# Dividing one early weight load and the input transpose before it in a TensorE-bound kernel

## The chip, the cores and the metric

The kernel runs on one core of one Trainium2 chip. The metric is the device time of one execution, in microseconds (us). The profile's span is the time from the first to the last recorded instruction of one profiled execution; here it is 1.3 to 1.4 us shorter than the device time of the same run.

## The reference

```python
g = sigmoid((x * gate_w).sum(-1))              # one gate per row
a = ssm(x)        # Bu = x @ B_bar^T (complex); h_t = Lam_bar*h_{t-1} + Bu_t; y = 2 Re(h @ C^T) + x*Dskip
b = gelu(x @ w1 + b1) @ w2 + b2
out = g * a + (1 - g) * b                      # x: 2048 x 640, w1: 640 x 1728, all bf16
```

For this change only `x @ w1` counts. The contraction length 640 is five row blocks of 128 (k = 0 to 4 in the code; the text counts them from one to five).

## The kernel before

The kernel works on four quarters of 512 rows. It opens with a pass of 42 matmuls over the first 1024 columns of W1, for the first quarter: all eight column blocks of row block one, then of row block two, and so on, into eight banks of PSUM, the memory that TensorE writes its results to. This order lets TensorE start as soon as the first row block of W1 and the first 128 columns of x are there, while the rest is still on its way. (The first two input blocks are loaded plainly and transposed on TensorE; the other three are transposed by DMA.) All of these loads are issued by one queue, SP, in this order:

```python
load("xna", "sp", "l_xna", ...)              # x, first two blocks, 256 KB
w1load(0, "sp", 1)                           # W1 row block one, 256 KB (128 x 1024)
w1load(1, "sp", 1.3)
xtrans(0, range(KN, KN + 1), 1.6, 0.8)       # DMA transpose of input block three, 128 KB
w1load(2, "sp", 2)
xtrans(0, range(KN + 1, KD), 3, 1.3)         # DMA transpose of input blocks four and five, 256 KB
w1load(3, "sp", 4)                           # W1 row block four
w1load(4, "sp", 5)                           # W1 row block five
# ... then: columns 1024 to 1727 of W1 in two parts ("w1_r0", "w1_r1"), the two B transposes, ...
```

The first pass asks for row block k only when it gets there:

```python
seq = [(k, jf) for k in range(KD) for jf in range(NW)]          # NW = 8 column blocks
# ... two small exceptions in the order of row blocks one and two cut ...
for k, jf, h in steps:
    op(f"m1_0_{jf}_{k}_{t0}", "pe", d_mm(t1 - t0), XK0[k] + [("w1", k)], [("bank", jf)], f_mm, ...)
```

Ahead of it, seven matmuls on a constant ("warm") and eight small transposes on TensorE are run.

## Time and profile before

| what | value | view |
|---|---|---|
| time | 213.02 us (212.69 to 213.04, 3 runs) | times |
| span of the profiled run | 211.5 us | page |
| TensorE busy | 208.6 us, 99% | page, part 1 |
| chain of waits that ended last | 99% TensorE | page, part 4 |
| TensorE's only stop in the first pass | 0.5 us ahead of one weight load | waits |

From the page of the kernel before: busy time by engine, the DMA row of the 40 slices (each digit is the busy share in tenths), and the shares of the chain that ended last.

```profile
PE 208.6 (99%) x1102; PEld 104.7 (50%) x1102; DVE 190.1 (90%) x240; ACT 103.3 (49%) x177; POOL 4.2 (2%) x12
...
DMA  6999999999400020063364000006752000005251
...
PE 99%; DVE 0%; issue 0%
```

TensorE is the limit. The DMA engines are nearly full for the first quarter of the run (ten of 40 slices) and have room in most of what follows, so the opening is the place to look for a late load.

The waits of TensorE's weight loads between 5 and 25 us, kernel before (total us, times, longest):

```profile
PEld ps L631 <- issue: 0.5, 1, 0.5
```

The chain that ended last, in order of time (start, us, what), kernel before. L407 are the warm-up matmuls, L419 the transposes on TensorE, L631 the first pass, L653 the following W1 matmuls, L696 the B projection:

```profile
0.78 2.93 PE ps L407 x7
3.71 0.03 issue
3.74 1.04 PE ps L419 x8
4.78 2.56 PE ps L631 x13
7.34 0.06 PE ps L438
7.40 2.81 PE ps L631 x13
10.20 0.06 issue
10.27 3.61 PE ps L631 x16
13.88 5.40 PE ps L653 x25
19.27 10.79 PE ps L696 x50
```

Row blocks four and five are the last 16 matmuls of L631. They start after a stop. Nothing on the later lines of this stretch stops TensorE again. The queue's issues in that stretch (start, us it took, instruction; L333 is a plain load, L340 a DMA transpose):

```profile
3.70 0.64 SPq L333 DMA_DIRECT2D W1sb<-in_B_w_dram  x1
4.38 1.26 SPq L340 DMA_TRANSPOSE xT<-in_A_x_dram  x1
5.69 2.10 SPq L333 DMA_DIRECT2D W1sb<-in_B_w_dram  x4
7.83 6.58 SPq L340 DMA_TRANSPOSE BT<-in_A_B_re_dram  x1
```

The two-block transpose takes 1.26 us of the queue, and row block four is the first of the four loads behind it.

### The profile page before, as it was taken

What the parts mean: (1) busy time and instruction counts of PE and PEld (TensorE: products, weight loads), DVE (VectorE), ACT (ScalarE), POOL (GpSimd) and SP (SyncE); (2) the same over time, 40 slices, a digit from 0 to 9 for tenths busy, and PEclk for the clock granted to TensorE, in tenths of its full rate; (3) what the DMA queues carried; (4) which work ended last, traced back from release to release, by engine and by line L of the source; (5) the groups of instructions that cost most, each with busy time, mean ns of one, the idle gap of its engine ahead of it and who ended that gap; (6) DMA issues with size and microseconds to landing.
All of it is one profiled execution on the core that took longest, in us unless ns stands there. A gap on an engine that the chain in (4) does not pass through costs nothing.

```text
span 211.5 us, 2743 instructions
## 1 busy us (share of the span) xinstructions
PE 208.6 (99%) x1102; PEld 104.7 (50%) x1102; DVE 190.1 (90%) x240; ACT 103.3 (49%) x177; POOL 4.2 (2%) x12
## 2 busy tenths in 40 slices
PE   8999999999999999999999999999999999999996
PEld 4444444444564444444464444444456444567775
DVE  2599999999999998999999999899999999499744
ACT  2489556679850353556680063456660037623330
POOL 1000000120000000000010000000010000000000
DMA  6999999999400020063364000006752000005251
GB/s 169 273 257 181 159 201 282 309 184 224 83 0 3 0 50 0 0 117 76 58 55 118 3 0 0 0 2 112 98 106 108 0 3 0 0 0 105 68 140 64
DMA packets 48424, 19.08 MB, mean 90 GB/s; under 512 B 41372, under 2 KB 47132, under 8 KB 48412
## 3 DMA queue, kind: packets, MB, share of 16 engines
q1 hardware_dynamic: 46752, 17.59, 39.1%
q0 software_dynamic: 1600, 1.32, 4.4%
q8 instruction: 8, 0.13, 0.3%
q10 hardware_dynamic: 60, 0.01, 0.1%
q14 instruction: 4, 0.03, 0.1%
HBM read 8.41 MB, written 2.63 MB: 52 GB/s over the span
## 4 chain that ended last, share of the span: by engine, by line
PE 99%; DVE 0%; issue 0%
PE ps L653 22%; PE ps L696 20%; PE ps L920 20%; PE ps L969 15%; PE ps L783 7%; PE ps L832 5%; PE ps L631 4%; PE ps L407 1%; PE ps L674 1%; PE ps L931 1%; PE ps L419 0%; PE ps L797 0%; DVE W1sb L866 0%; PE ps L438 0%
## 5 line engine op out<-in xcount | busy, mean ns | idle before, releaser
L653 PE MATMUL ps<-xT,W1sb 128*128 128x512 bf16 x220 | 48.1, 379 | 0.0
L736 DVE TENSOR_TENSOR_SCAN W<-atab,V 128x1280 bf16<-128x1280 f32 x16 | 44.3, 2811 | 0.3
L696 PE MATMUL ps<-xT,BT 128*128 128x512 bf16 x200 | 43.8, 379 | 0.0
L920 PE MATMUL ps<-Gl,W2sb 128*128 128x512 bf16 (+1 forms) x234 | 42.7, 344 | 0.0
L660 ACT ACTIVATE Gl<-ps,cols 128x512 bf16<-128x512 f32 x44 | 29.9, 694 | 15.5 <-PE ps L653 15.5
L653 PEld LDWEIGHTS ps<-xT,W1sb 128*128 128x128 bf16 x220 | 21.5, 98 | 26.0
L969 PE MATMUL ps<-Hb,CT 128*128 128x512 bf16 x150 | 32.9, 379 | 0.0
L920 PEld LDWEIGHTS ps<-Gl,W2sb 128*128 128x128 bf16 x234 | 22.9, 98 | 19.3
L705 ACT ACTIVATE U<-ps 128x512 bf16<-128x512 f32 x40 | 23.7, 596 | 15.6 <-PE ps L696 15.6
L696 PEld LDWEIGHTS ps<-xT,BT 128*128 128x128 bf16 x200 | 19.5, 98 | 23.8 <-ACT Gt L682 0.4
L938 ACT ACTIVATE E1T<-ps,cols 128x512 bf16<-128x512 f32 (+1 forms) x18 | 9.5, 624 | 36.0 <-PE ps L931 36.0
L969 PEld LDWEIGHTS ps<-Hb,CT 128*128 128x128 bf16 x150 | 14.4, 98 | 18.0 <-DVE Hb L488 0.3
L977 ACT ACTIVATE E2T<-ps 128x512 bf16<-128x512 f32 x15 | 9.1, 604 | 13.6 <-PE ps L969 13.6
L783 PE MATMUL ps<-W2sb,Gl 128*128 128x320 bf16 x104 | 14.8, 299 | 0.0
L606 DVE SCALAR_TENSOR_TENSOR trf<-xn,gwb 128x640 bf16<-128x640 bf16 x16 | 13.2, 823 | 0.4
L488 DVE TENSOR_TENSOR Hb<-Hb,V 128x1280 bf16<-128x1280 bf16 x16 | 12.5, 821 | 0.3
L488 DVE TENSOR_TENSOR V<-V,W 128x1280 bf16<-128x1280 bf16 x16 | 12.5, 821 | 0.3
L488 DVE TENSOR_TENSOR V<-mr,U 128x2560 bf16<-128x2560 bf16 x8 | 11.9, 1492 | 0.3
L783 PEld LDWEIGHTS ps<-W2sb,Gl 128*128 128x128 bf16 x104 | 10.1, 98 | 4.3 <-issue 0.3
L488 DVE TENSOR_TENSOR Hb<-c,W 128x2560 bf16<-128x2560 bf16 x8 | 11.9, 1491 | 0.2
L488 DVE TENSOR_TENSOR V<-s,W 128x2560 bf16<-128x2560 bf16 x8 | 11.9, 1484 | 0.0
L488 DVE TENSOR_TENSOR W<-mi,U 128x2560 bf16<-128x2560 bf16 x8 | 11.9, 1484 | 0.0
(91 smaller groups left out, 150.6 us busy)
## 6 DMA issues: line engine op xcount, KB each, us to landing
W2sb<-in_B_w_dram SPq DMA_DIRECT2D x1, 2080.0 KB, 9.1
out_dram<-xn SPq DMA_DIRECT2D x3, 640.0 KB, 4.8
W1sb<-in_B_w_dram SPq DMA_DIRECT2D x5, 256.0 KB, 4.2
xn<-in_A_x_dram POOLq DMA_DIRECT2D x2, 640.0 KB, 7.4
trf<-grow SPq DMA_DIRECT2D x3, 256.0 KB, 5.1
xn<-in_A_x_dram SPq DMA_DIRECT2D x1, 640.0 KB, 7.3
W1sb<-in_B_w_dram SPq DMA_DIRECT2D x1, 480.0 KB, 5.6
out_dram<-W1sb SPq DMA_DIRECT2D x3, 160.0 KB, 1.8
```

What stands on the lines that cost most here:

```text
L488: return inc("dve", nc.vector.tensor_tensor(out=o, in0=a, in1=b, op=o_))
L606: t = inc("dve", nc.vector.scalar_tensor_tensor(out=scr[:, :], in0=xn[q % 2][:, c, :], scalar=1.0, in1=gwb[:, :], op0=ALU.mult, op1=ALU.mu ...
L653: t = nc.tensor.matmul(PS[bank][:, :], W1sb[:, k, jf * 128:(jf + 1) * 128], xT[q][:, k, :], start=(k == 0), stop=(k == KD - 1))
L660: return inc("act", nc.scalar.activation(Gl[q % 2][:, jf, :], PS[bank][:, :], ACT.Gelu_apprx_tanh, bias=b1col[:, jf:jf + 1]))
L696: t = nc.tensor.matmul(PS[bank][:, :], BT[:, ci, kd, k * 128:(k + 1) * 128], xT[q][:, kd, :], start=(kd == 0), stop=(kd == KD - 1))
L705: return inc("act", nc.scalar.activation(dst, src, ACT.Copy, scale=1.0 if ci == 0 else -1.0))
L736: t = inc("dve", nc.vector.tensor_tensor_scan(out=g[:, ci, :], data0=a, data1=v[:, ci, :], initial=0.0, op0=ALU.mult, op1=ALU.add))
L783: t = nc.tensor.matmul(PS[bank][:, 0:HALF], Gl[q % 2][:, jf, t4 * 128:(t4 + 1) * 128], W2sb[:, jf, cols], start=False, stop=False, skip_gr ...
L832: t = nc.tensor.matmul(PS[bank][:, 0:n], H[b % NHB][:, ci, k, s * 128:(s + 1) * 128], CT[:, ci, k, cols], start=(i == 0), stop=(i == 2 * K ...
L920: t = nc.tensor.matmul(PS[bank][:, 0:t1 - t0], W2sb[:, jf, d * 128:(d + 1) * 128], Gl[q % 2][:, jf, t0:t1], start=(jf == 0), stop=False)
L938: return inc("act", nc.scalar.activation(E1T[:, d, t0:t1], PS[bank][:, 0:t1 - t0], ACT.Identity, bias=cols2[:, 0, d:d + 1]))
L969: t = nc.tensor.matmul(PS[bank][:, :].rearrange("p (s t) -> p s t", s=2), CT[:, ci, k, d * 128:(d + 1) * 128], Hb[:, 2 * (q % 2):2 * (q % ...
```

## The change

The intent: TensorE should not wait for row block four. Input block five, which is not needed before row block five, moves behind row block four, and row block four comes in two loads, so that its first six column blocks can start on the first 192 KB.

```diff
-        xtrans(0, range(KN + 1, KD), 3, 1.3)
-        w1load(3, "sp", 4)
+        xtrans(0, range(3, 4), 3, 0.8)
+        FS = 6 * 128
+        for i, (f0, f1) in enumerate(((0, FS), (FS, FW))):
+            load(f"w1_3{i}", "sp", f"l_w13{i}", W1sb[:, 3, f0:f1], B_w1[3 * 128:4 * 128, f0:f1],
+                 [("w1", 3, i)], prio=4 + 0.2 * i, lat=2.6)
+        xtrans(0, range(4, 5), 4.5, 0.8)
         w1load(4, "sp", 5)
+        def w1tok(k, jf):
+            return ("w1", k, int(jf * 128 >= FS)) if k == 3 else ("w1", k)
```

The readers of W1 then wait for `w1tok(k, jf)` instead of `("w1", k)`. Nothing else changes; in the two traces the order of instructions on TensorE, VectorE and ScalarE is the same, and the queue has two DMA issues more (48 against 46; the prediction's "38 rows to 41" is not what the traces show).

More of the change, by code (lines that the diff above doesn't have):

```diff
@@ L366, in bass_gated_mix__ssm_conv_s5__dense_activation_gelu__prompt_kernel @@
         w1load(2, "sp", 2)
-        xtrans(0, range(KN + 1, KD), 3, 1.3)
-        w1load(3, "sp", 4)
+        xtrans(0, range(3, 4), 3, 0.8)
+        FS = 6 * 128
+        for i, (f0, f1) in enumerate(((0, FS), (FS, FW))):
+            load(f"w1_3{i}", "sp", f"l_w13{i}", W1sb[:, 3, f0:f1], B_w1[3 * 128:4 * 128, f0:f1], [("w1", 3, i)], prio=4 + 0.2 * i, lat=2.6)
+        xtrans(0, range(4, 5), 4.5, 0.8)
         w1load(4, "sp", 5)
+        def w1tok(k, jf):
+            return ("w1", k, int(jf * 128 >= FS)) if k == 3 else ("w1", k)
         FM = FW + 3 * 128
@@ L632, in f_mm @@
                                                       start=(k == 0 and t0 == 0), stop=(k == KD - 1), skip_group_check=jf < 2))
-                op(f"m1_0_{jf}_{k}_{t0}", "pe", d_mm(t1 - t0), (XK0[k] if h is None else XK0[k][h:h + 1]) + [("w1", k)], [("bank", jf)],
+                op(f"m1_0_{jf}_{k}_{t0}", "pe", d_mm(t1 - t0), (XK0[k] if h is None else XK0[k][h:h + 1]) + [w1tok(k, jf)], [("bank", jf)],
                    f_mm, prio=pe_prio())
@@ L655, in f_mm @@
                     return inc("pe", t)
-                m1op[q] = op(f"m1_{q}_{jf}", "pe", KD * d_mm(512), XT[q] + ([("w1", k) for k in range(KD)] if jf < NW else [("w1", "r", int(jf * 128 >= FM))]), [("bank", bank)], f_mm, prio=pe_prio())
+                m1op[q] = op(f"m1_{q}_{jf}", "pe", KD * d_mm(512), XT[q] + ([w1tok(k, jf) for k in range(KD)] if jf < NW else [("w1", "r", int(jf * 128 >= FM))]), [("bank", bank)], f_mm, prio=pe_prio())
                 def f_ge(jf=jf, bank=bank):
```

## The prediction

> What bounds the kernel. The chain of waits that ended last is 99% TensorE, busy 208.6 of 211.5 us. One 128x512 matmul ends every 0.216 us (matmul ends in the timeline). So only a gap in TensorE's stream is worth anything. VectorE (90% busy) holds TensorE up nowhere in the middle, so a shift at the start should reach the end in full.
>
> What the change aims at. The first pass over W1 (42 matmuls) has one gap: in the wait view the weight load ahead of row block four idles 0.53 us until 10.23 us ("issue", here a DMA wait). Part is ordinary spacing, part hidden by the matmul in flight: the matmul ends are 0.438 us apart instead of 0.216. The true loss is 0.22 us, 0.1% of the run. The gap ends with the landing of W1's fourth row block: its sixteen completion increments come at 9.03 to 10.13 us, twelve by 9.08; one engine is late (a 2 KB packet took 1.13 us). The transpose of input blocks four and five had landed at 8.46. The Trainium skill, page "DMA: Bandwidth & Descriptors", section "Why a DMA increments its semaphore by 16 and not by 1", says that only the full 16 means that all data landed; the trace agrees (9.08 did not release TensorE, 10.13 did).
>
> What the change does. Instruction order on TensorE, VectorE and ScalarE stays; only the DMA issue queue changes, 38 rows to 41. The two-block transpose becomes two of one block, with 192 KB and 64 KB of row block four between them. Ahead of the end of the first needed piece lie 128 + 64 KB less, at that stretch's 270 GB/s an estimated 0.7 us. So that piece should land at about 9.4 us, before TensorE wants it (9.8), and the gap should close.
>
> What it costs. The one-block transpose already there takes 1.20 us to issue, the two-block one 1.26; a short load 0.4 to 0.6. So the queue gets an estimated 1.2 to 1.7 us longer before row block five: issued at 7.5 to 8.1 instead of 6.31, it lands at 10.8 to 11.5 instead of 10.78, against a need at about 11.45. The rest of W1 (landed 12.38, needed about 13.3) and the first B transpose (landed 17.53, needed about 18.7) slip too, by less than the issue delay: the DMA engines are about 90% busy from 5 to 25 us, and issue runs 1 to 2 us ahead of data. Some transposes show a pause of 0.6 to 1.3 us on many engines (ending at 5.75, at 13.35); one more transpose may bring one more.
>
> Sum: -0.22 us if the gap closes; 0 to +0.6 if a new one opens before row block five, the rest of W1 or B. Expected -0.1 us on a run whose three times differ by 0.35 us. Predicted 212.9 us, range 212.3 to 213.8. Chances: faster by over 2% 0.005, within 2% 0.985, slower 0.01.
>
> What would show each step. Right: no gap over 0.3 us between matmul ends in the first pass; row block four's first part landed before 9.8; first pass ending 0.2 us earlier; later stages shifted alike. Wrong: a wait before row block five at about 11.5, the second W1 part at 13.5 or the B projection at 19; or transposes that issue in 0.6 us each, so that nothing slips.
>
> What would make it wrong: another late packet (luck of one engine) on row block four or five; a VectorE limit that takes back the gain; noise larger than the effect.

## The result, and the profile after

The changed kernel took 212.8 us (median of 6 runs, 212.38 to 213.29), the kernel before 212.89 us (6 runs, 212.51 to 213.39). The ratio is 0.9996, with a 95% interval of 0.9977 to 1.0015: the same. A ratio here is the mean time of one kernel's fast runs over that of the other's of the same rounds, so it is not quite the ratio of the medians. A second set of six runs of the changed kernel gave 0.9997 (0.9965 to 1.003), where one run of the kernel before at 214.92 us widens the interval.

The profiled run was 211.03 us long, 0.45 us shorter than that of before (211.48). The chain that ended last, changed kernel (L414 warm-up, L426 transposes on TensorE, L638 first pass, L660 the next W1 matmuls, L703 the B projection):

```profile
0.74 2.88 DMA xn<-in_A_x_dram
3.63 0.05 issue
3.67 0.30 PE ps L426 x2
3.97 0.02 issue
4.00 0.50 DVE xT L432 x2
4.50 2.62 PE ps L638 x13
7.11 0.06 PE ps L445
7.17 6.26 PE ps L638 x29
13.43 5.40 PE ps L660 x25
18.82 10.79 PE ps L703 x50
```

The stop before row block four is gone: the last 29 matmuls of the first pass now run in one piece of 6.26 us, where before they took 2.81 + 0.06 + 3.61 = 6.48 us. That is the 0.22 us that was aimed at. But the B projection starts 19.27 - 18.82 = 0.45 us earlier, so a second 0.23 us came from elsewhere: it is there already at the L445/L438 line (7.34 against 7.11), ahead of any matmul that the change touches. The stretch before it shows why. TensorE between 3.6 and 4.6 us, kernel before (start, us, instruction):

```profile
3.74 1.04 PE L419 MATMUL ps<-ident,xn 128*128 128x128 bf16 x8
```

and the changed kernel:

```profile
3.67 0.62 PE L426 MATMUL ps<-ident,xn 128*128 128x128 bf16 x8
```

The same eight transposes took 1.04 us in one run and 0.62 us in the other. Their ends are 0.107 us apart in the first and 0.056 in the second: TensorE still ran at half rate in the one and already at full rate in the other. The Trainium skill, page "TensorE: Matmul & The Clock Gate", section "Part 1: The HAM clock gate (the "warmup" mystery)", describes this: a cold array runs at half clock until about 3.4 us of activity have been seen in a window that is not aligned to the kernel's start, so the moment differs from run to run. These two traces agree on the half rate and on the moment that differs, but not on the 3.4 us: in the changed kernel's profile full rate was there at about 3.5 us, 2.7 us after the first matmul (0.78). The packed trace of this run has a clock record too: 1.0 from 3.40 us on. (Nine of the twelve traces have one, from 3.40 to 4.46 us; this profile of the kernel before has none, and its matmul ends put the moment at about 5.2.) The change has no part in this: up to 4.38 us both kernels issue the same to TensorE and to the queue. The first x load, which the transposes wait for, also landed 0.07 us earlier in this run (3.63 against 3.69).

The waits of weight loads between 5 and 25 us, changed kernel:

```profile
PEld ps L638 <- DMA W1sb<-in_B_w_dram: 0.4, 1, 0.4
PEld ps L445 <- issue: 0.2, 1, 0.2
```

The wait that is left is ahead of row block two, which landed at 6.03 us; it costs 0.10 us (matmul ends 0.312 instead of 0.216 us apart), and it is there because the earlier clock brought TensorE to it sooner. The queue, changed kernel:

```profile
3.69 0.63 SPq L333 DMA_DIRECT2D W1sb<-in_B_w_dram  x1
4.38 1.13 SPq L340 DMA_TRANSPOSE xT<-in_A_x_dram  x1
5.55 1.05 SPq L333 DMA_DIRECT2D W1sb<-in_B_w_dram  x2
6.65 1.12 SPq L340 DMA_TRANSPOSE xT<-in_A_x_dram  x1
7.82 1.63 SPq L333 DMA_DIRECT2D W1sb<-in_B_w_dram  x3
9.49 5.58 SPq L340 DMA_TRANSPOSE BT<-in_A_B_re_dram  x1
```

A transpose of one block takes nearly as long to issue as one of two (1.13 and 1.12 against 1.26 us). So, with the one short load more (0.43 us), everything behind it is issued 1.66 us later (9.49 against 7.83), and row block five starts at 7.82 instead of 6.31.

The data pays as well. What the DMA engines moved between 8.8 and 9.4 us, shortly before the second transpose landed (9.87), is the last number of these lines of the windows view (GB/s; the one before it is the DMA share), kernel before and changed kernel:

```profile
8.80:9.40 0.60, 0.60 (x5) 0.25 (x4) 0.51 (x3) 0.60 (x1) 0.00 (x0) 1.00 1.16 348
8.80:9.40 0.60, 0.60 (x5) 0.25 (x4) 0.53 (x3) 0.60 (x1) 0.00 (x0) 1.00 1.00 98
```

The other profiles of the two kernels, introduced below, show the same: 331 to 382 GB/s before, 80 to 106 with the change. Whether the engines pause for the transpose or have too little issued to do, these views do not separate. The prediction had allowed that one more transpose may bring one more pause.

### The profile page after: what moved, and what is told of

Same layout as the page of the kernel before. It is cut to its first block, busy times and chain, and to the rows that moved or that the text cites. A ratio compares the mean times of both kernels' runs of the same rounds, so it can differ in the third digit from the quotient of the medians.

```text
span 211.0 us, 2746 instructions
## 1 busy us (share of the span) xinstructions
PE 208.0 (99%) x1102; PEld 104.2 (49%) x1102; DVE 190.1 (90%) x240; ACT 102.9 (49%) x177; POOL 4.2 (2%) x12
## 4 chain that ended last, share of the span: by engine, by line
PE 97%; DMA 1%; DVE 0%; issue 0%
PE ps L660 23%; PE ps L703 21%; PE ps L927 20%; PE ps L976 15%; PE ps L790 7%; PE ps L839 5%; PE ps L638 4%; DMA xn<-in_A_x_dram 1%; PE ps L681 1%; PE ps L938 1%; PE ps L804 0%; DVE xT L432 0%; DVE W1sb L873 0%; PE ps L426 0%; PE ps L445 0%
## 5 line engine op out<-in xcount | busy, mean ns | idle before, releaser
L660 PE MATMUL ps<-xT,W1sb 128*128 128x512 bf16 x220 | 48.1, 379 | 0.0
L703 PE MATMUL ps<-xT,BT 128*128 128x512 bf16 x200 | 43.8, 379 | 0.0
L660 PEld LDWEIGHTS ps<-xT,W1sb 128*128 128x128 bf16 x220 | 21.5, 98 | 26.0
L703 PEld LDWEIGHTS ps<-xT,BT 128*128 128x128 bf16 x200 | 19.5, 98 | 23.8 <-ACT Gt L689 0.4
```

What stands on the lines that cost most here:

```text
L660: t = nc.tensor.matmul(PS[bank][:, :], W1sb[:, k, jf * 128:(jf + 1) * 128], xT[q][:, k, :], start=(k == 0), stop=(k == KD - 1))
L703: t = nc.tensor.matmul(PS[bank][:, :], BT[:, ci, kd, k * 128:(k + 1) * 128], xT[q][:, kd, :], start=(kd == 0), stop=(kd == KD - 1))
```

## The experiments

Two questions are left. Was the 0.22 us a property of the queue's order, or chance of that one run? And what do the later issues cost? Run times cannot answer: they spread by 0.9 us, while the effect is 0.2. The profile can. Three rules are used below, all read from the traces.

- Lost time: in steady flow weight loads start 0.216 us apart. The lost time at a row block is the step by which this raster shifts there. This does not need the matmul records, of which 14 of 1102 are missing in the profiles of the experiments.
- A weight load is asked for while the matmul before is still in flight, so a little lateness is hidden: in the first profile the load before row block four started 0.41 us late and 0.22 us was lost, so 0.19 was hidden.
- "Landed" is the last of a load's sixteen completion increments; the weight load starts about 0.1 us later.

### Is the gap of the kernel before there every time, and what does each half of the change do?

On chip 6, as all experiments but two that are marked: the kernel before once more, each half of the change alone, and the changed kernel once more; all with one profile and no timing rounds.

The kernel before, unchanged:

> The kernel before, unchanged, once more. Theory A (queue order): row block four always lands too late behind two transposed blocks, so the gap before its first matmul comes back: the last of its sixteen increments between 9.9 and 10.3 us, matmul ends there 0.35 to 0.6 us apart instead of 0.216. Theory B (luck of one engine): twelve of the sixteen increments came by 9.08 us, so in another run the last one comes by about 9.3 and there is no gap. The end of the opening transposes (4.78 us in the first profile, 4.30 in the changed kernel's) should move from run to run by up to 0.5 us with the moment at which the TensorE clock doubles, in either theory.

The two-block transpose divided, row block four whole:

```diff
-        xtrans(0, range(KN + 1, KD), 3, 1.3)
+        xtrans(0, range(3, 4), 3, 0.8)
         w1load(3, "sp", 4)
+        xtrans(0, range(4, 5), 4.5, 0.8)
```

> Only the two-block input transpose is divided, row block four stays one 256 KB load between the halves. Theory A (queue order): the transpose half that is moved behind it is what frees row block four; it lands at about 9.2 to 9.4 us and the gap before it closes (matmul ends at most 0.25 us apart). Row block five lands at about 10.9 to 11.2. Rival (the load has to be cut): row block four whole lands at 9.7 us or later and leaves a gap of 0.05 us or more.

Row block four divided, the transpose whole and in front:

```diff
         xtrans(0, range(KN + 1, KD), 3, 1.3)
-        w1load(3, "sp", 4)
+        # two loads of 192 and 64 KB, waited for separately, as in the change
```

> Only the load of row block four is cut into 192 and 64 KB, both after the undivided two-block transpose. Theory A: the first part gains only the 64 KB behind it, an estimated 0.2 to 0.25 us at 270 GB/s, so it lands at 9.0 to 9.9 us depending on the late engine; the gap shrinks to between 0 and 0.1 us. Row block five lands at 10.9 to 11.2 (one more issue of 0.45 us). Rival (the cut alone does it): no gap and the first part at 8.8.

The changed kernel, unchanged:

> The changed kernel once more. No gap before row block four; its first part lands at 8.8 to 9.2 us. Row block five lands at 11.0 to 11.4 (11.23 in the first profile), within 0.1 us of the moment TensorE asks for it; a gap of up to 0.2 us there is possible. The second row block of W1 lands at about 6.0 and costs 0 to 0.15 us, more when the TensorE clock doubles early. Span 211.0 to 211.6 us.

Measured: with the divided transpose alone, row block four landed at 9.21 us and nothing was lost before it; row block five landed at 10.99. (It lost 0.17 us before row block two, which landed at 6.10 us; the change does not touch that.) With the divided load alone, the first part landed at 9.85, and 0.11 us was lost, a little more than expected; row block five landed at 10.73, earlier than expected. The weight loads of the first pass from 8 to 14 us, divided transpose alone and divided load alone:

```profile
7.94 5.06 PEld L632 LDWEIGHTS ps<-xT,W1sb 128*128 128x128 bf16 x24
...
7.93 1.61 PEld L637 LDWEIGHTS ps<-xT,W1sb 128*128 128x128 bf16 x8
9.95 3.15 PEld L637 LDWEIGHTS ps<-xT,W1sb 128*128 128x128 bf16 x16 [0.41 <-issue]
```

This looks as if moving input block five were what counts. But a landing mixes two things: when most of a load came, and how late its last engine was. By the twelfth increment the divided transpose alone was no earlier (9.19 us) than the kernel before (8.96 to 9.30 in the four profiles below); it lost nothing because its last increment came only 0.02 us later. The divided load alone had its twelfth at 8.90 and its last 0.95 us after it. Only both halves together are clearly earlier (8.19 to 8.66 in four profiles). With one profile of each half, which half frees row block four stays open.

The repeat of the changed kernel lost nothing at row blocks four and five, with a first part even earlier than expected (8.59), but the second W1 part (the first of the two loads of columns 1024 to 1727) landed at 13.23 us, and 0.06 us was lost before it: a new small stop behind the longer queue.

The surprise is the kernel before. In its second profile row block four landed at 9.62, not after 9.9, and nothing was lost. The waits of weight loads in it still show a stop there:

```profile
PEld ps L631 <- issue: 0.3, 1, 0.3
...
```

but the weight load started only 0.15 us late, which is hidden behind the matmul in flight. The span was 211.0 us, the same as the changed kernel's.

### How often?

> The kernel before, a third profile, because the first two differ: row block four's last increment came at 10.13 us with 0.22 us of TensorE time lost in one and at 9.62 us with nothing lost in the other. Theory B (luck of one engine): the last increment anywhere between 9.2 and 10.2 us, 0.2 us or more after the twelfth of the sixteen, the loss between 0 and 0.25 us, and no other gap in the first pass over 0.1 us. Theory A (queue order alone): 9.9 us or later with a loss of 0.15 us or more, and the 9.62 of the second profile was the exception.

> As for the third profile of before. Over the four profiles theory B expects a mean loss before row block four of 0.05 to 0.15 us, theory A of 0.15 us or more.

> The changed kernel, a third profile, and six more times of each kernel. Row block four's first part lands at 8.5 to 9.2 us even with a late engine and nothing is lost before it. Lost time before the second W1 part (which landed at 12.68 and 13.23 us against a request at about 13.0) between 0 and 0.1 us, before row block five between 0 and 0.1. Ratio of the times 0.998 to 1.001: a mean gain of about 0.1 us in 213 is below what six runs resolve.

> As for the third profile of the changed kernel. Over its four profiles the mean loss in row blocks four, five and the second W1 part together is 0 to 0.08 us.

Worked out from the eight profiles (an ordinary table; times in us; "asked" is when the weight load would have started without a wait):

```
kernel before             profile 1   2       3       4       mean
twelfth of 16 increments     9.08    9.27    8.96    9.30
row block four landed       10.13    9.62    9.99    9.32
row block four asked         9.83    9.58    9.48    9.62
lost before row block four   0.224   0.001   0.428   0.001   0.16
row block five landed       10.78   10.86   10.68   11.02
second W1 part landed       12.38   12.29   11.98   12.37
first B transpose landed    17.53   17.22   16.80   17.21
span                       211.48  211.01  211.34  211.04  211.22

changed kernel            profile 1   2       3       4       mean
first part of four landed    9.06    8.59    8.68    8.68
lost before row block four   0.000   0.000   0.000   0.001   0.00
row block five landed       11.23   11.10   10.85   11.44
row block five asked        11.32   11.29   11.91   11.22
lost before row block five   0.001   0.001   0.001   0.138   0.04
second W1 part landed       12.68   13.23   12.56   12.77
lost before second W1 part   0.001   0.063   0.001   0.001   0.02
first B transpose landed    17.95   17.97   18.08   18.03
span                       211.03  211.05  211.63  211.07  211.20
```

The third profile of before has the stop again, longer; its waits between 5 and 25 us:

```profile
PEld ps L631 <- issue: 0.7, 1, 0.7
...
```

and the fourth profile of the changed kernel has one before row block five (0.14 us, where up to 0.1 was expected). Its weight loads from 8 to 14 us (start, us, instruction, idle before):

```profile
7.99 3.12 PEld L638 LDWEIGHTS ps<-xT,W1sb 128*128 128x128 bf16 x15
11.55 1.42 PEld L638 LDWEIGHTS ps<-xT,W1sb 128*128 128x128 bf16 x8 [0.44 <-issue]
13.09 0.96 PEld L660 LDWEIGHTS ps<-xT,W1sb 128*128 128x128 bf16 x5
```

Neither theory holds alone. The mean loss of 0.16 us falls on theory A's side, but A asked for a loss each time. The queue's order puts most of row block four at 9.0 to 9.3 us, ahead of the request at 9.5 to 9.8: on its own this loses nothing, as the second and fourth profiles show. In the first and third profiles the last increment came about 1.0 us after the twelfth, and only then was time lost. How much depends also on when TensorE gets there: the third profile lost 0.43 us, more than theory B allowed, because TensorE asked early (9.48). An early clock was not the reason: its clock record starts at 4.43 us, later than in the second and fourth profiles (3.84 and 4.05). Its first x load and its row block two had landed earlier than in those (3.59 against 3.77 and 3.76; 5.74 against 5.94 and 5.90). So the gap is real but comes and goes, 0 to 0.43 us, with a mean of 0.16 over four profiles. The change removed it in all four of its profiles, although its first part had late engines too (the last increment 0.02 to 0.59 us after the twelfth): the first part comes early enough to hide them. (An estimate: with the largest lateness seen, 1.05 us, it would land at 9.2 to 9.7 us, against requests at 9.50 to 10.19; only in the fourth profile would it come after its request.) It lost 0.05 us on average at two later places instead. The net is an estimated 0.11 us, from four profiles each, or 0.05% of the run. This is too small for the times to show. The mean spans differ by less still (211.22 and 211.20), because the third profile of the changed kernel had its clock doubled late. Why engines come late in some runs stays open: the trace that I have does not say which engine an increment belongs to. The packet of 1.13 us that the prediction names ended at 9.31 us, so at most it put its engine behind, and in the third profile no packet in that stretch took over 0.6 us, yet the last increment was as late.

### How much room is left behind the change?

```diff
         xtrans(0, range(4, 5), 4.5, 0.8)
+        load_T("dup", "l_dup", [(E2T[:, 0:1, :], x2[0:512, 4 * 128:5 * 128])], [("E2T", 0)], 4.7, 0.8)
         w1load(4, "sp", 5)
```

> The changed kernel with one more one-block transpose (into a buffer that is used much later) ahead of row block five: the suspected cost doubled. Theory (no slack left before row block five): row block five is issued 1.1 to 1.2 us later and lands at 12.0 to 12.4 us instead of 11.23; a gap opens before it of 0.6 to 1.0 us of lost TensorE time, and the end comes as much later as the first pass ends later: 0.5 to 1.0 us over the changed kernel. The rest of W1 and the first B transpose may add up to 0.5 us each. Rival (the DMA engines are the limit and the issue queue is ahead): it lands by 11.6 and less than 0.2 us is lost.

Measured on chip 8, with 5 rounds: 213.75 us (213.61 to 214.39) against 212.73 of before; ratio 1.0039 (1.0006 to 1.0073). The weight loads from 9 to 21 us show two stops:

```profile
9.00 2.26 PEld L639 LDWEIGHTS ps<-xT,W1sb 128*128 128x128 bf16 x11
12.26 1.42 PEld L639 LDWEIGHTS ps<-xT,W1sb 128*128 128x128 bf16 x8 [1.00 <-issue]
13.79 5.28 PEld L661 LDWEIGHTS ps<-xT,W1sb 128*128 128x128 bf16 x25
20.09 0.98 PEld L704 LDWEIGHTS ps<-xT,BT 128*128 128x128 bf16 x6 [1.02 <-DMA BT<-in_A_B_re_dram]
```

Row block five was issued 1.30 us later than in the first profile of the changed kernel (9.12 against 7.82; I had said 1.1 to 1.2), landed at 12.15 us, and 0.70 us was lost, as the theory said. The first B transpose landed at 20.05, and a second 0.70 us was lost there; I had allowed 0.5. The rival falls. Row block five landed 0.92 us later than in the first profile of the changed kernel; the 128 KB in front of it alone would take an estimated 0.5 us at the kernel before's 270 GB/s, but that rate did not hold here: the windows view gives 80 GB/s from 8.8 to 9.4 us and 67 from 10.0 to 10.6, a second dip. How much is issue and how much is data, this run does not separate. The change stands near an edge: one more transpose of this kind loses 1.40 us in the profile, and 1.0 us against before in the median times, which is still within 2%.

### Does a loss at the start reach the end in full?

This needs no run of its own. From the weight load of the fifth matmul of the B projection (at 19.76 us in the first profile of before) to the end of the span takes 191.72, 191.71, 191.72 and 191.72 us in the four profiles of before, 191.72, 191.71, 191.73 and 191.72 in those of the changed kernel, and 191.72 with one transpose more. Over all twelve profiles it lies between 191.70 and 191.73. Everything that differs between these profiles is in the first 20 us, and passes to the end unchanged. From the last matmul of row block one to that point takes 13.65 us plus what is lost on the way. The last matmul of row block one itself has its weight load at 5.54 to 6.25 us, a spread of 0.7 us, larger than anything that this change moves. Two causes are visible. In the nine profiles with a clock record (3.40 to 4.46 us) it is at 5.54 to 5.71, always 1.86 to 1.95 us after the landing of the first x load (3.59 to 3.79). In the three others, where the matmul ends show the clock doubling at about 4.9 to 5.8 us, it comes 2.1 to 2.5 us after that landing.

### Both moved, nothing divided

```diff
-        xtrans(0, range(KN + 1, KD), 3, 1.3)
-        w1load(3, "sp", 4)
+        w1load(3, "sp", 3)
+        xtrans(0, range(KN + 1, KD), 4, 1.3)
```

> From the kernel before, the load of row block four and the two-block transpose change places, nothing is divided, the queue has as many rows as before. Theory A: both land before 9.7 us (the load at about 8.6 to 8.9, the transpose at about 9.1 to 9.6), so the gap before row block four closes, and row block five keeps its time of before, 10.5 to 10.8 us, with 0.5 us or more of slack. The time is 0.1 to 0.5 us under that of before, inside the noise: ratio 0.998 to 1.0005. Rival (a transpose is followed by a pause, or must come early): the transpose lands after 9.8 us and the gap stays, then because of it.

Measured on chip 8, with 5 rounds: 213.03 us (212.4 to 215.07) against 212.73 of before (212.23 to 214.89); ratio 1.0021 (0.9974 to 1.0067): within 2%, above the expected ratio (at most 1.0005), and no better than before as far as this can tell. One run of each kernel near 215 us widens the interval; no profile caught one. In the profile, the load landed at 8.54 and the transpose at 9.57 us, and nothing was lost anywhere in the first pass. Row block five landed at 10.93, later than expected (10.5 to 10.8) and about 0.35 us ahead of what TensorE needed, with less slack than I expected (0.5) but with no more issues in the queue than before. Row block three lost its slack too: it landed at 7.87 us, against 7.17 to 7.68 in the four profiles each of the other two kernels, and its weight load started 0.04 us late, which was hidden. So this may be a simpler way to the same effect, but it is one profile, and its times show no gain over the kernel before.

## Why the prediction was right, point by point

That the time fell into the range says little by itself: the whole effect is 0.1 to 0.2 us, and the range (212.3 to 213.8) holds all six times of the kernel before as well. What counts is the mechanism.

- TensorE bounds the run, and a shift at the start reaches the end in full: right. The rest of the run after 20 us was 191.70 to 191.73 us in all twelve profiles. VectorE took nothing back.
- The gap closes: right in all four profiles of the changed kernel. The first part of row block four landed at 8.6 to 9.1 us; I had said about 9.4. The estimate of 0.7 us saved fits the twelfth increments (means 9.15 and 8.38 us); the late engine adds the rest. I had reckoned from 10.13 us, the landing with the latest engine of the four profiles.
- The size of the gain, "The true loss is 0.22 us": right for that profile, wrong as the kernel's typical loss. Four profiles show 0.22, 0.00, 0.43 and 0.00. I read the late engine from the trace, named its luck, and yet took its result as the gain. That the expected total of -0.1 us agrees with the estimated net of -0.11 is partly accident.
- The queue grows by 1.2 to 1.7 us: right (1.66). Row block five issued at 7.82 (said 7.5 to 8.1) and landed at 10.85 to 11.44 (said 10.8 to 11.5), and "nearly no slack" was right: in two of four profiles it landed 0.09 and 0.19 us before it was asked for, of which about 0.1 us goes to the start of the weight load, and in one 0.14 us was lost. One transpose more lost 0.70 us there.
- The later loads slip "by less than the issue delay": right. Means over four profiles: second W1 part from 12.26 to 12.81, first B transpose from 17.19 to 18.01, so 0.55 and 0.82 us against 1.66. "One more transpose may bring one more" pause was right as well, in the DMA rate: 80 to 106 GB/s from 8.8 to 9.4 us, against 331 to 382.
- "First pass ending 0.2 us earlier": the profile showed 0.45. The other 0.23 was ahead of the change: the clock doubling earlier in that run and 0.07 us from the first x load, less 0.10 lost before row block two. "No gap over 0.3 us between matmul ends" failed by a hair, at a place that the change does not touch: 0.312 before row block two, again because TensorE was early.
- Not foreseen: the moment of clock doubling and the landing of the first x load as the largest sources of spread in the opening, and their trade with the DMA waits. Part of an early start can be lost again at the next load (0.10 us before row block two in the first profile of the changed kernel, 0.43 before row block four in the third of before), and a late one hides late loads (third profile of the changed kernel, no loss anywhere).

## What to carry to other kernels

When one engine is busy for 99% of the run, a change at the start is worth only the idle time that it removes there; read that as the spacing of the matmul ends, not as the idle time of the weight loads, part of which is hidden. Before such a gap is called a property of the kernel, take the profile of the same kernel again: here 0.22 us was 0.00, 0.43 and 0.00 in the next three. When each half of a change has a single profile, compare more than the last increment before one half is given the credit. And when a load is moved forward in a queue, look at what stands behind it: a divided transpose costs nearly a second full issue, and the next loads pay for it.

## What the Trainium skill lacked or had wrong

- "TensorE: Matmul & The Clock Gate", Part 1, gives about 500 ns either way as the run-to-run variation of the clock's doubling, although a note in the same part counts 6, 11 or 14 slow matmuls in runs of one kernel, which is more. In these twelve profiles of nearly the same opening the change of matmul spacing falls between 3.5 us (changed kernel, first profile, in the last warm-up matmul) and 5.8 us (its third profile, in the fifth matmul of the first pass), worked out from the matmul ends: a spread of 2.3 us. The explanation by an unaligned window is compatible with such a spread; the figure of 500 ns is not. The figure of about 3.4 us of activity is not met either: the earliest change came 2.7 us after the first matmul.
- "DMA: Bandwidth & Descriptors" gives sequencer cycles per transpose instruction of small tiles for earlier generations, but no measured issue time for one of a few blocks. Here the issue record was 1.12 to 1.26 us for one block of 512 x 128 and 1.25 to 1.57 us for two: far from proportional to the size.
- The same page, section "Why a DMA increments its semaphore by 16 and not by 1", says that the engines finish independently. It does not say by how much they differ. Here the last engine came between 0.02 and 1.05 us after the twelfth in the same load of the same kernel.
- No page says how much lateness of a weight load is hidden by the matmul in flight. Here it was 0.19 us of 0.41, and 0.19 us of 0.88, behind 128x512 matmuls.
